# Table columns in PSUM, seven raw and eleven split weight buffers, and a lighter share of the weight splits for GpSimd

## The chip, the cores and the metric

The kernel runs on one core of a Trainium2 chip. The metric is device microseconds of one execution, from the launch of the program on the chip to its end, inputs and outputs in HBM. Before the change three runs took 615.19, 617.08 and 616.91 us, so the median is 616.91 us. The five engines of the core are called by the profile's names: PE (matrix multiply; PEld is its weight load), DVE (vector), ACT (scalar), POOL (GpSimd) and SP (which here only issues DMAs).

## The reference: what is computed

A linear attention feeds a mixture of experts. Cut to what matters:

```
q, k, v: (8 batches, 8 heads, 576 positions, 64); w_phi: (64, 128), all float32
phi(x)  = proj = x @ w_phi; proj -= max|proj| over its 128 features; [exp(proj), exp(-proj)]
attn    = phi(q) @ (phi(k)^T v) / (phi(q) . sum phi(k) + 1e-6)
x       = attn as (4608 tokens, 512)
compute = x @ w_skip > 0            # the other tokens are copied to the output
logits  = x[compute] @ w_gate       # 8 experts; expert = argmax, weight = softmax at the argmax
y       = weight * (relu(x @ w1[expert]) @ w2[expert])      # w1: 512 x 1024, w2: 1024 x 512
out     = x + y for computed tokens, x for the others       # (4608, 512) float32
```

## The kernel before, in words

**First stage, 0 to about 342 us.** The attention, batch after batch. It also writes every token's row with its gate weight to DRAM (`xrows`) and sorts the tokens by expert (one-hot rows `OH`, ranks `RKH`, and position patterns `OP`). The change doesn't touch its code.

**Second stage, the experts.** The tokens of an expert are cut into slots, each a piece of matrix work with its own expert. There are three early full slots "E" of 256 rows (their experts are picked before the last batch is known), full slots "D" of 256 rows, "C" slots of 192 rows and "S" slots of 128 rows, in the order `('E','E','E','C','C','SC','C','DS','C','D')`; in "SC" and "DS" two slots are interleaved. A slot has two layers and each layer's weights come in four **chunks** of 128 x 1024 float32 (512 KB), so there are 96 chunks, numbered 0 to 95 in the order in which PE uses them: 0 to 23 are the three E slots, 24 to 39 two C slots, 40 to 55 the SC pair (40 to 43 the S slot's first layer, 44 and 45 half of the C slot's first layer, 46 to 49 the S slot's second layer, 50 to 55 the rest of C), 56 to 63 a C slot, 64 to 79 the DS pair, 80 to 87 a C slot and 88 to 95 the last D slot.

**The way of one chunk.** (1) `fetch` (L184, L187) issues the DMA on SP's queue into a **raw buffer** `wraw_c`. (2) `split` makes two float32r halves so that PE can multiply at its fast rate without losing accuracy: ACT copies raw to `hi` (L195), then DVE or POOL writes `lo = raw - hi` (L200) into a **split buffer** `w`. DVE does a chunk in one instruction of 1024 columns, POOL in four of 256. (3) PE multiplies with `hi` and `lo`: L932 (hi), L933 (hi with the token's low half `xl`) and L935 (lo) in the first layer of a full slot, L946, L950 (lo) and L951 in its second; L919 and L922 (lo) in a C slot's first layer; L848, L849 (lo), L850 and L869, L870 (lo), L871 in an S slot. There are 11 raw buffers (the first 12 chunks use four of them) and 9 split buffers. A raw buffer is free for the next load when ACT and the `lo` engine have read it, a split buffer when PE has used it.

**Who splits.** ACT makes every `hi`. For `lo`, POOL takes a fixed list of the E chunks (`gp`: 0, 1, 2, 4, 6, 8, 9, 11, 12, 14, 17, 19, 21), chunks 1 and 3 of a C slot's first layer, and chunks 1 and 3 of each layer of an S slot. DVE takes all others. POOL's queue also issues the gathers of token rows (L213) and the scatters of output rows (L879).

**What sets the order.** The code of the second stage stands under a manual schedule: each engine runs in the order of the Python calls. At step k the loop first calls `part` (the split) for all chunks up to a reach of k+5 whose estimated time is due, and after each split the `load` of the chunk 11 further on. Then come PE's matmuls of chunk k, then ReLU and the `hlo` half of the hidden activations (L824 and L825; for C slots L924, L925 `hsum`, L834, L836), and the work that is hung on the step by `at`: the row gathers, the transposes of gathered rows with their halves `xh` (L809) and `xl` (L810), the stores (L893 with the row index L878, L904, L905), and pieces of `tables`. The estimates `ready`, `parted` and `T` only steer this placing.

**The tables.** `tables` computes which token goes to which slot, on DVE, in pieces at the steps 5 to 32. For each of 36 token tiles it has small columns (128 partitions x 36): `pe`, rank `rk`, the three coefficients `cc`, `lt`, and the column `col`. From `col` four comparisons make `eq` (L1061, 128 x 558), and PE multiplies them with `OP` (L1050) to the index table in the PSUM bank K. All of these columns lie in SBUF.

Of the kernel before, what the change touches and what calls it, by code (L numbers as in the profile page):

```python
# [8 lines left out]
F32 = mybir.dt.float32  # L9
F32R = mybir.dt.float32r  # L10
BF16 = mybir.dt.bfloat16
I32 = mybir.dt.int32
AF = mybir.ActivationFunctionType
ALU = mybir.AluOpType
AX = mybir.AxisListType
# [3 lines left out]
P = 128  # L19
# [5 lines left out]
def kernel(  # L25
# [91 lines left out]
    eid0 = const.tile([1, 3], I32, name="eid0")  # L117
    idg0 = const.tile([P, 3, 2], I32, name="idg0")
    pad0 = const.tile([P, 3, 2], I32, name="pad0")
    const.tile([1, 40], I32, name="spare")  # L120
    mark = const.tile([1, 32], I32, name="mark")[:, 0:1]

    ft = const.tile([P, NSL, 4], I32, name="ft")
# [51 lines left out]
    def fetch(which, wap, c):  # L175
        i = nchunk[0]

        j = i % 4 if i < 12 else (i - 8) % 11
        rawp = wpool[0 if j < 4 else 3]
        nchunk[0] += 1  # L180
        raw = rawp.tile([P, 1024], F32, tag="wraw%d" % j, name="wraw_c", bufs=1)
        if which == 1:
            src = wap[:, :, c * FC:(c + 1) * FC].rearrange("o (k p) f -> p (o k) f", p=P)
            nc.sync.dma_start(out=raw.rearrange("p (k f) -> p k f", f=FC), in_=src)  # L184
        else:
            src = wap[:, c * FC:(c + 1) * FC, :].rearrange("o (k p) m -> p (o k) m", p=P)
            nc.sync.dma_start(out=raw.rearrange("p (k m) -> p k m", m=DM), in_=src)  # L187
        return which, i, raw

    def split(chunk, eng):  # L190
        which, i, raw = chunk
        s = i % 9
        pair = wpool[1 if s < 4 else 2].tile([P, 2, 1024], F32R, tag="w%d" % s, name="w", bufs=1)
        hi, lo = pair[:, 0], pair[:, 1]
        nc.scalar.activation(out=hi, in_=raw, func=AF.Copy)  # L195

        n = 256 if eng is nc.gpsimd else 1024
        for a in range(0, 1024, n):
            r = slice(a, a + n)
            eng.tensor_tensor(out=lo[:, r], in0=raw[:, r], in1=hi[:, r].bitcast(F32), op=ALU.subtract)  # L200
        w = FC if which == 1 else DM
        return hi.rearrange("p (k f) -> p k f", f=w), lo.rearrange("p (k f) -> p k f", f=w)
# [761 lines left out]
    start = {"E": 0, "D": 0, "C": NSD, "S": NS2}  # L964

    def tables():
        cn = bank("K")[:, 0:E]
        nc.tensor.matmul(cn, ones_b, Stot, start=True, stop=True)
        yield
        ni = const.tile([P, E], I32, name="ni")  # L970
# [40 lines left out]
        nc.vector.tensor_tensor(out=cf[:, 2], in0=cf[:, 2], in1=cf[:, 1], op=ALU.subtract)  # L1011

        rk = const.tile([P, NT], F32, name="rk")
        pe = const.tile([P, NT], F32, name="pe")
        tm = const.tile([P, NT, E], F32, name="tm")
        cc = const.tile([P, 3, NT], F32, name="cc")
        col = const.tile([P, NT], F32, name="col")
        lt = const.tile([P, NT], F32, name="lt")
        pk = const.tile([P, E], F32, name="pk")

# [8 lines left out]
        nc.vector.tensor_reduce(out=pe, in_=tm, axis=AX.X, op=ALU.add)  # L1029
        nc.vector.scalar_tensor_tensor(out=rk, in0=pe, scalar=-2.0, in1=RKH, op0=ALU.mult, op1=ALU.add)  # L1030
        yield
        for c in range(3):
            nc.vector.tensor_tensor(out=tm, in0=OH, in1=per_e(cf[:, c], NT), op=ALU.mult)
            nc.vector.tensor_reduce(out=cc[:, c], in_=tm, axis=AX.X, op=ALU.add)
        yield
        nc.vector.tensor_tensor(out=lt, in0=rk, in1=cc[:, 1], op=ALU.is_lt)
        nc.vector.tensor_tensor(out=col, in0=cc[:, 0], in1=cc[:, 2], op=ALU.subtract)
        nc.vector.tensor_tensor(out=col, in0=col, in1=lt, op=ALU.mult)
        nc.vector.tensor_tensor(out=col, in0=col, in1=cc[:, 2], op=ALU.add)
        nc.vector.tensor_tensor(out=col, in0=col, in1=rk, op=ALU.add)  # L1040
        nc.vector.scalar_tensor_tensor(out=col, in0=rk, scalar=0.0, in1=col, op0=ALU.is_ge, op1=ALU.mult)
        ix = bank("K")[:, 0:NCOL]
        C = 9
        rxs = []

# [98 lines left out]
    took = {"E": 2.85, "D": 2.85, "C": 2.4, "S": 1.45}  # L1144
    T, ready, parted = [], [], []
    for k, (w, x, c) in enumerate(steps):
        arrive = 0.0 if k < FIRST else max(ready[k - 1] + (3.0 if k < 12 else 2.35), parted[k - (4 if k < 12 else 11)] + 4.0)
        ready.append(arrive)
        parted.append(max(arrive, T[k - 9] + 3.0 if k >= 9 else 0.0, parted[k - 1] + 1.25 if k else 0.0))
        T.append(max(T[k - 1] + took[steps[k - 1][1][0]] + (1.0 if w == 1 and c == 0 else 0.0) if k else 2.0,  # L1150
                     parted[k] + 2.5))

# [39 lines left out]
    with tc.manual_schedule():  # L1192
# [4 lines left out]
        for k, (w, x, c) in enumerate(steps):  # L1197
            kind, i = x
            for f in [f for s, f in before if s == k]:
                f()  # L1200
            tabled[0] = kind != "E"
            todo = [f for s, f in along if s == k]
            while nxt < len(steps) and nxt <= k + 5 and (nxt <= k + 1 or parted[nxt] <= T[k] + 1.0):
                w_, x_, c_ = steps[nxt]
                v = nxt not in CFG["gp"] if x_[0] == "E" else not (
                    (x_[0] == "C" and w_ == 1 or x_[0] == "S") and c_ % 2 == 1)
                part(nxt, nc.vector if v else nc.gpsimd)
                for n in (range(nxt + 4, nxt + 5) if nxt < 7 else range(11, 19) if nxt == 7 else range(nxt + 11, nxt + 12)):
                    load(n)
                nxt += 1  # L1210
            if w == 1:
                if kind == "S":
                    st = hss.setdefault(x, {})
                    half1(wts[k], xss[x], c, st)
                    if c % 2 == 1:
                        st[c // 2] = half1_out(st[c // 2], c // 2)

                        def turn(st=st, g=c // 2):
                            st[g] = half1_turn(st[g])
                        at(k + 1, turn)  # L1220
                else:
                    hss.setdefault(x, []).append(mm1(wts[k], xss[x]))
            else:
                if c == 0:
                    ys[x] = [bank("O") for _ in range(1 if kind == "S" else 2)]
                if kind == "S":
                    half2(wts[k], ys[x][0], hss[x], c)
                elif x != last:
                    mm2(wts[k], ys[x], xss[x], hss[x], c)
                elif c == NFC - 1:  # L1230
                    for sub in range(2):
                        for cc in range(NFC):
# [12 lines left out]
            for s, f in [a for a in along if a[0] == k and a[1] not in todo]:
                f()
# [47 lines left out]
```

## Time and profile before

| | before |
|---|---|
| median of 3 runs | 616.91 us (615.19 to 617.08) |
| the profiled execution, time | 617.51 us |
| the profiled execution, span from first to last instruction | 615.8 us |
| granted TensorE clock, mean | 0.984 |
| attention, about 0 to 342 us; expert slots to the last matmul | PE from 343.1 to 605.8 us |
| PE busy | 571.6 us, 93% |
| DVE, POOL, ACT busy | 509.9, 381.5, 331.0 us |
| weight loads | 96 of 512 KB, median 5.2 us from issue to landing |

How to read it: the span is that of one execution that the profiler recorded, and the execution took 1.7 us more than its span. PE's busy time counts a matmul from start to its modelled end, so that a busy PE is not yet a PE at its peak rate; what an engine waits for is read from the idle times in front of its instructions. In the timeline rows a number stands for the start in us, the next for the duration in us (of all instructions merged in the row, with their count as x4 and the like), then engine, line, operation, the tile written and the tiles read, and shapes; a bracket at the end has the idle time before and what ended it. The duration of a DVE or POOL instruction runs from the end of its semaphore waits, so it contains whatever else holds it up.

### The profile page before, as it was taken

What the parts mean: (1) busy time and instruction counts of PE and PEld (TensorE: products, weight loads), DVE (VectorE), ACT (ScalarE), POOL (GpSimd) and SP (SyncE); (2) the same over time, 40 slices, a digit from 0 to 9 for tenths busy, and PEclk for the clock granted to TensorE, in tenths of its full rate; (3) what the DMA queues carried; (4) which work ended last, traced back from release to release, by engine and by line L of the source; (5) the groups of instructions that cost most, each with busy time, mean ns of one, the idle gap of its engine ahead of it and who ended that gap; (6) DMA issues with size and microseconds to landing.
All of it is one profiled execution on the core that took longest, in us unless ns stands there. A gap on an engine that the chain in (4) does not pass through costs nothing. (4 is left out here: it accounts for less than half of the span.)

```text
span 615.8 us, 18780 instructions
## 1 busy us (share of the span) xinstructions
PE 571.6 (93%) x7486; PEld 467.4 (76%) x7486; DVE 509.9 (83%) x1081; ACT 331.0 (54%) x649; POOL 381.5 (62%) x415
## 2 busy tenths in 40 slices
PE   4899999999999999998899799789999799999993
PEld 2577777767777677776667789588889589989892
DVE  5899999999989999999997679967688877956851
ACT  3465556556655555655544454334658556666620
POOL 5665585494855967667754756855467983559121
PEclk9899999999999999999999899999999899999997
DMA  9998888987677766423153499577686599597200
GB/s 157 160 157 150 186 184 178 196 184 142 134 162 160 160 114 155 119 73 113 37 160 127 136 338 341 170 275 228 216 263 203 178 297 327 175 318 238 76 19 30
DMA packets 250234, 108.34 MB, mean 176 GB/s; under 512 B 192417, under 2 KB 235553, under 8 KB 250144
## 3 DMA queue, kind: packets, MB, share of 16 engines
q1 hardware_dynamic: 245632, 97.58, 60.7%
q0 software_dynamic: 3200, 9.45, 4.5%
q8 instruction: 60, 0.98, 0.7%
q10 hardware_dynamic: 1312, 0.08, 0.1%
q14 instruction: 30, 0.25, 0.1%
HBM read 83.86 MB, written 24.02 MB: 175 GB/s over the span
## 5 line engine op out<-in xcount | busy, mean ns | idle before, releaser
L200 POOL TENSOR_TENSOR w<-wraw_c,w 128x256 fp32r<-128x256 f32 x124 | 109.8, 920 | 42.1 <-ACT w L195 36.0
L380 POOL TENSOR_TENSOR z<-ek 128x512 f32<-128x512 f32 x64 | 81.2, 1273 | 77.0 <-ACT ek L373 54.1
L195 ACT ACTIVATE w<-wraw_c 128x1024 fp32r<-128x1024 f32 x96 | 97.6, 1052 | 3.8 <-DMA wraw_c<-in_moe_w_dram 3.5
L200 DVE TENSOR_TENSOR w<-wraw_c,w 128x1024 fp32r<-128x1024 f32 x65 | 87.8, 1359 | 13.9 <-ACT w L195 12.8
L354 DVE TENSOR_REDUCE m<-ps_P 128x8 f32<-128x1024 f32 (+2 forms) x86 | 88.6, 1030 | 7.1 <-PE ps_P L347 7.1
L357 DVE TENSOR_TENSOR u<-ps_P,m 128x1024 f32<-128x1024 f32 (+2 forms) x86 | 88.8, 1033 | 2.9
L347 PE MATMUL ps_P<-wsrc,xT 64*64 64x128 f32 x2048 | 79.3, 283 | 11.7 <-DMA raw<-in_k_dram 7.1
L513 PEld LDWEIGHTS ps_O<-kva,eq 128*64 128x64 f32 x2048 | 74.0, 136 | 16.3 <-issue 5.8
L513 PE MATMUL ps_O<-kva,eq 128*64 128x74 f32 x2048 | 77.4, 228 | 3.8 <-DVE lgm L476 3.7
L347 PEld LDWEIGHTS ps_P<-wsrc,xT 64*64 64x64 f32 x2048 | 57.4, 135 | 28.2 <-issue 20.3
L399 ACT ACTIVATE eq<-ps_U 128x512 f32<-128x512 f32 x64 | 37.9, 593 | 64.7 <-PE ps_U L393 64.2
L415 PE MATMUL ps_K<-ek,v 128*64 128x256 f32 x512 | 72.0, 400 | 0.0
L879 POOL DMA_INDIRECT out_dram<-o,si x22 | 28.8, 1309 | 66.8 <-DVE si L878 60.4
L946 PE MATMUL ps_O<-w,hh 128*128 128x512 f32 x160 | 64.1, 401 | 0.0
L633 POOL TENSOR_SCALAR OP<-iota_p,rkp,wcol 128x128 bf16<-128x128 f32 x62 | 48.4, 790 | 24.0 <-DVE RKH L636 17.8
L372 ACT ACTIVATE ek<-u 128x512 f32<-128x512 f32 x64 | 40.5, 633 | 38.7 <-DVE u L357 22.8
L950 PE MATMUL ps_O<-w,hh 128*128 128x512 f32 x120 | 47.8, 398 | 3.5 <-DVE w L200 2.9
L393 PE MATMUL ps_U<-ident,u 128*128 128x128 f32 x288 | 48.9, 287 | 1.0 <-DVE u L357 0.6
L324 DVE STREAM_TRANSPOSE xT<-raw 128x512 f32<-128x512 f32 x64 | 44.7, 701 | 5.9 <-PE ps_P L347 2.6
L415 PEld LDWEIGHTS ps_K<-ek,v 128*64 128x64 f32 x512 | 32.1, 138 | 21.5 <-issue 11.3
L951 PE MATMUL ps_O<-w,hlo 128*128 128x512 f32 x120 | 47.6, 397 | 0.1
L384 POOL TENSOR_TENSOR z<-z 128x512 f32<-128x512 f32 x32 | 40.8, 1274 | 2.5
(253 smaller groups left out, 1214.1 us busy)
## 6 DMA issues: line engine op xcount, KB each, us to landing
wraw_c<-in_moe_w_dram SPq DMA_DIRECT2D x96, 512.0 KB, 5.2
raw<-in_k_dram SPq DMA_DIRECT2D x64, 144.0 KB, 3.1
raw<-in_q_dram SPq DMA_DIRECT2D x64, 144.0 KB, 4.1
v<-in_v_dram SPq DMA_DIRECT2D x64, 128.0 KB, 2.8
out_dram<-xm SPq DMA_DIRECT2D x16, 512.0 KB, 4.2
xrows<-xm SPq DMA_DIRECT2D x8, 516.0 KB, 4.1
xrows<-xm SPq DMA_DIRECT2D x8, 512.0 KB, 4.4
vt<-in_v_dram SPq DMA_DIRECT2D x32, 32.0 KB, 2.6
```

What stands on the lines that cost most here:

```text
L195: nc.scalar.activation(out=hi, in_=raw, func=AF.Copy)
L200: eng.tensor_tensor(out=lo[:, r], in0=raw[:, r], in1=hi[:, r].bitcast(F32), op=ALU.subtract)
L347: nc.tensor.matmul(p[s * 64:s * 64 + 64, hd, (nj + j) * NF:(nj + j + 1) * NF], xT[r, g * P + s * 64:g * P + s * 64 + 64], wsrc[r], start=T ...
L354: nc.vector.tensor_reduce(out=m.rearrange("p (j h) -> p j h", h=2), in_=pv, axis=AX.X, op=ALU.max, apply_absolute_value=True)
L357: nc.vector.tensor_tensor(out=uu[:, 0:2 * nj, :].rearrange("p (j h) f -> p j h f", h=2), in0=pv, in1=m.rearrange("p (j h o) -> p j h o", h ...
L380: zeng.tensor_tensor(out=z, in0=e[:, 0:2, :], in1=e[:, 2:4, :], op=ALU.add)
L393: nc.tensor.transpose(t[:, tt * P:(tt + 1) * P], uu[:, tt, :], ident)
L415: nc.tensor.matmul(o[hd * 64:hd * 64 + 64, :], u.v[:, 2 * hd + pr, g * D:(g + 1) * D], u.e[i][:, 2 * j + hd, :], start=(g == 0), stop=False,)
L513: nc.tensor.matmul(ov[s * 64:s * 64 + 64, 2 * j + hd, :], e[:, half, j, hd, s * 64:s * 64 + 64], kva[:, half, 2 * pr + hd, :], start=(half ...
L633: (nc.vector if last else nc.gpsimd).tensor_scalar(out=OP[:, t0 + t, c, :], in0=iota_p, scalar1=rkp[:, t:t + 1], scalar2=wcol[:, NT:NT + 1 ...
L946: nc.tensor.matmul(y[sub], hh[:, t], wh[:, fi, :], start=first, stop=False)
L950: nc.tensor.matmul(y[sub], hh[:, t], wl[:, fi, :], start=False, stop=False)
```

## The change

Four things are changed, in the second stage alone.

1. **Table columns.** `tables` keeps its PSUM bank K for its whole run and places `pe`, `col` and the first two coefficients (`c0`, `c1`, before `cc[:, 0]` and `cc[:, 1]`) in it, next to the counts and the index table. `rk`, `lt` and the third coefficient `c2` stay in SBUF. The operations on them and their order are the same.
2. **Buffers.** Raw buffers go from 11 to 7, split buffers from 9 to 11. The load that follows the split of chunk n is that of chunk n+7 instead of n+11. The memory for both together stays the same (11 x 4 KB + 9 x 8 KB = 7 x 4 KB + 11 x 8 KB = 116 KB in each partition).
3. **Reach.** The split of a chunk may be placed up to six steps ahead of PE instead of five, and the estimates are made for the new numbers of buffers.
4. **Shares.** In an S slot POOL makes `lo` for chunk 1 of each layer only; chunk 3 goes to DVE. With two S slots of two layers that is four chunks of 96.

A spare tile of the constants grows from 40 to 64 words, so that everything behind it lies 512 bytes lower than before.

```diff
@@ fetch, split
-        j = i % 4 if i < 12 else (i - 8) % 11
+        j = i % 4 if i < 12 else (i - 8) % 7
-        s = i % 9
+        s = i % 11
@@ tables
-        cn = bank("K")[:, 0:E]
+        kb = bank("K")
+        cn = kb[:, 0:E]
...
-        pe = const.tile([P, NT], F32, name="pe")
+        ix = kb[:, E:E + NCOL]
+        pe, col, c0, c1 = (kb[:, a:a + NT] for a in range(E + NCOL, E + NCOL + 4 * NT, NT))
         tm = const.tile([P, NT, E], F32, name="tm")
-        cc = const.tile([P, 3, NT], F32, name="cc")
-        col = const.tile([P, NT], F32, name="col")
+        c2 = const.tile([P, NT], F32, name="c2")
...
-        for c in range(3):
+        for c, cc in enumerate((c0, c1, c2)):
             nc.vector.tensor_tensor(out=tm, in0=OH, in1=per_e(cf[:, c], NT), op=ALU.mult)
-            nc.vector.tensor_reduce(out=cc[:, c], in_=tm, axis=AX.X, op=ALU.add)
+            nc.vector.tensor_reduce(out=cc, in_=tm, axis=AX.X, op=ALU.add)
@@ the loop over the steps
-            while nxt < len(steps) and nxt <= k + 5 and (nxt <= k + 1 or parted[nxt] <= T[k] + 1.0):
+            while nxt < len(steps) and nxt <= k + 6 and (nxt <= k + 1 or parted[nxt] <= T[k] + 1.0):
                 v = nxt not in CFG["gp"] if x_[0] == "E" else not (
-                    (x_[0] == "C" and w_ == 1 or x_[0] == "S") and c_ % 2 == 1)
+                    x_[0] == "C" and w_ == 1 and c_ % 2 == 1 or x_[0] == "S" and c_ == 1)
-                for n in (range(nxt + 4, nxt + 5) if nxt < 7 else range(11, 19) if nxt == 7 else range(nxt + 11, nxt + 12)):
+                for n in (range(nxt + 4, nxt + 5) if nxt < 7 else range(11, 15) if nxt == 7 else range(nxt + 7, nxt + 8)):
                     load(n)
```

The order in which the engines run shows where this lands. On DVE, in the stretch of the tables (the first `w` is the split of chunk 13, `hlo` belongs to the second E slot), before:

```order
L1029 TENSOR_REDUCE pe<-tm 128x36
L1030 SCALAR_TENSOR_TENSOR rk<-pe,RKH 128x36
L200 TENSOR_TENSOR w<-wraw_c,w 128x1024
L825 SCALAR_TENSOR_TENSOR hlo<-ps_P,hh 128x512
L1033 TENSOR_TENSOR tm<-OH,cf 128x288
```

and now:

```order
L1030 TENSOR_REDUCE ps_K<-tm 128x36
L1031 SCALAR_TENSOR_TENSOR rk<-ps_K,RKH 128x36
L200 TENSOR_TENSOR w<-wraw_c,w 128x1024
L825 SCALAR_TENSOR_TENSOR hlo<-ps_P,hh 128x512
L1034 TENSOR_TENSOR tm<-OH,cf 128x288
```

No row moves here, nor in the rest of this stretch up to the last `eq`: the same operations follow each other, and only where a column is read and written changes.

On POOL, in the SC pair, before (a row `w` is a chunk of four pieces: 41 and 43, behind the two scatters L879 45, and behind the two gathers L213 47, 49 and 51):

```order
L200 TENSOR_TENSOR w_7715<-wraw_c_7368,w_7715 128x256 x4
L200 TENSOR_TENSOR w_7758<-wraw_c_7438,w_7758 128x256 x4
L879 DMA out_0_dram<-o_7791,si_7793 4608x512
L888 MEMSET mark_129 1x1
L879 DMA out_0_dram<-o_7800,si_7804 4608x512
L888 MEMSET mark_129 1x1
L200 TENSOR_TENSOR w_7810<-wraw_c_7500,w_7810 128x256 x4
L213 DMA xg_7874<-xrows_93,ft_130 128x514
L213 DMA xg_7876<-xrows_93,ft_130 64x514
L200 TENSOR_TENSOR w_7878<-wraw_c_7548,w_7878 128x256 x4
L200 TENSOR_TENSOR w_7927<-wraw_c_7615,w_7927 128x256 x4
L200 TENSOR_TENSOR w_8005<-wraw_c_7685,w_8005 128x256 x4
```

and now (chunks 41, 45, 47 and 51):

```order
L200 TENSOR_TENSOR w_7676<-wraw_c_7468,w_7676 128x256 x4
L200 TENSOR_TENSOR w_7767<-wraw_c_7576,w_7767 128x256 x4
L879 DMA out_0_dram<-o_7785,si_7787 4608x512
L888 MEMSET mark_129 1x1
L879 DMA out_0_dram<-o_7794,si_7798 4608x512
L888 MEMSET mark_129 1x1
L200 TENSOR_TENSOR w_7837<-wraw_c_7646,w_7837 128x256 x4
L213 DMA xg_7859<-xrows_93,ft_130 128x514
L213 DMA xg_7861<-xrows_93,ft_130 64x514
L200 TENSOR_TENSOR w_7960<-wraw_c_7755,w_7960 128x256 x4
```

Chunks 43 and 49 have left POOL, and chunk 45 stands before the two scatters, chunk 47 before the two gathers; each stood behind them. On DVE chunks 43 and 49 stand behind chunks 42 and 48, and from chunk 22 on a split stands in front of the work of the step before the one in which it stood (before, DVE ran split 46 behind the two `xl` of the C slot of the pair, now ahead of them).

More of the change, by code (lines that the diff above doesn't have):

```diff
@@ L119 @@
     pad0 = const.tile([P, 3, 2], I32, name="pad0")
-    const.tile([1, 40], I32, name="spare")
+    const.tile([1, 64], I32, name="spare")
     mark = const.tile([1, 32], I32, name="mark")[:, 0:1]
@@ L1031, in tables @@
         yield
-        for c in range(3):
+        for c, cc in enumerate((c0, c1, c2)):
             nc.vector.tensor_tensor(out=tm, in0=OH, in1=per_e(cf[:, c], NT), op=ALU.mult)
-            nc.vector.tensor_reduce(out=cc[:, c], in_=tm, axis=AX.X, op=ALU.add)
+            nc.vector.tensor_reduce(out=cc, in_=tm, axis=AX.X, op=ALU.add)
         yield
-        nc.vector.tensor_tensor(out=lt, in0=rk, in1=cc[:, 1], op=ALU.is_lt)
-        nc.vector.tensor_tensor(out=col, in0=cc[:, 0], in1=cc[:, 2], op=ALU.subtract)
+        nc.vector.tensor_tensor(out=lt, in0=rk, in1=c1, op=ALU.is_lt)
+        nc.vector.tensor_tensor(out=col, in0=c0, in1=c2, op=ALU.subtract)
         nc.vector.tensor_tensor(out=col, in0=col, in1=lt, op=ALU.mult)
-        nc.vector.tensor_tensor(out=col, in0=col, in1=cc[:, 2], op=ALU.add)
+        nc.vector.tensor_tensor(out=col, in0=col, in1=c2, op=ALU.add)
         nc.vector.tensor_tensor(out=col, in0=col, in1=rk, op=ALU.add)
         nc.vector.scalar_tensor_tensor(out=col, in0=rk, scalar=0.0, in1=col, op0=ALU.is_ge, op1=ALU.mult)
-        ix = bank("K")[:, 0:NCOL]
         C = 9
@@ L1146 @@
     for k, (w, x, c) in enumerate(steps):
-        arrive = 0.0 if k < FIRST else max(ready[k - 1] + (3.0 if k < 12 else 2.35), parted[k - (4 if k < 12 else 11)] + 4.0)
+        arrive = 0.0 if k < FIRST else max(ready[k - 1] + (3.0 if k < 12 else 2.35), parted[k - (4 if k < 12 else 7)] + 4.0)
         ready.append(arrive)
-        parted.append(max(arrive, T[k - 9] + 3.0 if k >= 9 else 0.0, parted[k - 1] + 1.25 if k else 0.0))
+        parted.append(max(arrive, T[k - 11] + 3.0 if k >= 11 else 0.0, parted[k - 1] + 1.25 if k else 0.0))
         T.append(max(T[k - 1] + took[steps[k - 1][1][0]] + (1.0 if w == 1 and c == 0 else 0.0) if k else 2.0,
```

## The prediction

> **What bounds the kernel now.** I read the page's sums first, then who PE waits for in the expert stage, then busy time and clock by stretch, then the timelines of PE, DVE and POOL where PE waits.
>
> ```profile
> span 615.8 us, 18780 instructions
> PE 571.6 (93%) x7486; PEld 467.4 (76%) x7486; DVE 509.9 (83%) x1081; ACT 331.0 (54%) x649; POOL 381.5 (62%) x415
> ```
>
> PE is the bound as a whole, so only time in which it waits or runs at a lower clock can be won. PE's waits from 320 us on (total us, times, longest):
>
> ```profile
> PE ps_O L870 <- POOL w L200: 3.2, 3, 1.4
> PE ps_O L950 <- DVE w L200: 2.9, 1, 2.9
> PE ps_P L919 <- DVE hsum L925: 2.1, 4, 1.0
> PE ps_P L933 <- DVE x L810: 1.7, 1, 1.7
> PE ps_O L950 <- POOL w L200: 0.6, 1, 0.6
> PE ps_P L935 <- POOL w L200: 0.5, 2, 0.3
> PE ps_P L922 <- POOL w L200: 0.3, 1, 0.3
> ```
>
> They lie in two places. Busy time by stretch (us, PE, PEld, DVE, ACT, POOL, then the granted clock):
>
> ```profile
> 380.00:392.00 12.00, 10.87 (x53) 8.48 (x52) 11.76 (x14) 5.22 (x6) 11.51 (x14) 1.00 0.72 224
> 392.00:404.00 12.00, 7.30 (x31) 5.39 (x30) 11.90 (x14) 2.98 (x4) 6.34 (x7) 0.86 0.54 176
> 468.00:480.00 12.00, 11.68 (x91) 11.15 (x90) 10.61 (x14) 9.50 (x17) 11.47 (x14) 1.00 0.63 203
> 480.00:496.00 16.00, 12.79 (x58) 10.26 (x59) 13.55 (x16) 7.73 (x12) 15.51 (x15) 0.89 0.65 218
> ```
>
> In 380 to 404 us, the tables, DVE has not half a microsecond to spare. In 480 to 496, the SC pair, it is POOL. In both the clock falls behind the waits: 12 x 0.14 = 1.7 us and 16 x 0.11 = 1.8 us lost. Now the tables' stretch, on DVE, POOL and PE:
>
> ```profile
> 378.54 5.57 DVE L1030 SCALAR_TENSOR_TENSOR rk<-pe,RKH 128x36 f32<-128x36 f32 x1
> 384.03 1.21 DVE L200 TENSOR_TENSOR w<-wraw_c,w 128x1024 fp32r<-128x1024 f32 x1
> 389.23 0.68 DVE L825 SCALAR_TENSOR_TENSOR hlo<-ps_P,hh 128x512 fp32r<-128x512 f32 x1
> 389.82 0.33 DVE L1036 TENSOR_TENSOR lt<-rk,cc 128x36 f32<-128x36 f32 x1
> 392.97 0.66 DVE L1041 SCALAR_TENSOR_TENSOR col<-rk,col 128x36 f32<-128x36 f32 x1
> 393.66 1.19 DVE L1061 TENSOR_TENSOR eq<-i,col 128x558 bf16<-128x558 f32 x1
> 394.77 1.75 DVE L200 TENSOR_TENSOR w<-wraw_c,w 128x1024 fp32r<-128x1024 f32 x1
> 397.04 0.72 DVE L1061 TENSOR_TENSOR eq<-i,col 128x558 bf16<-128x558 f32 x1
> 401.78 1.28 DVE L810 TENSOR_TENSOR x<-ps_U,x 128x512 fp32r<-128x512 f32 x2
> ...
> 378.48 5.57 POOL L200 TENSOR_TENSOR w<-wraw_c,w 128x256 fp32r<-128x256 f32 x8
> 387.41 10.93 POOL L200 TENSOR_TENSOR w<-wraw_c,w 128x256 fp32r<-128x256 f32 x12
> ...
> 396.57 0.50 PE L950 MATMUL ps_O<-w,hh 128*128 128x512 f32 x1 [2.92 <-DVE w L200]
> 403.12 0.38 PE L933 MATMUL ps_P<-x,w 128*128 128x256 f32 x1 [1.68 <-DVE x L810]
> ```
>
> An operation on 36 columns needs 5.57 us, as long as POOL's eight pieces (chunks 11 and 12) run, and ends with them. From 389.82 to 393.66 six such operations take 3.84 us, 0.64 each, with POOL's pieces beside them (10.93 / 12 = 0.91 each). The split of chunk 15 (394.77) is late by this, PE waits 2.92 us for it, and `xl` of the third slot (401.78) is late next. Every slow operation reads two operands in SBUF; `hlo`, which reads ps_P, stays at 0.68.
>
> **Part 1, the columns.** Two rows give the price of a small operation without such a wait, one with a PSUM operand and one with SBUF operands:
>
> ```profile
> 368.93 0.14 DVE L980 SCALAR_TENSOR_TENSOR cl<-pks,ps_K 128x8 f32<-128x8 f32 x1
> 370.62 0.17 DVE L984 SCALAR_TENSOR_TENSOR rm_e<-nn,cl 128x8 f32<-128x8 f32 x1
> ```
>
> Writing a small column to PSUM isn't shown; I bound it by 0.14 and, for a whole 128x512 from PSUM, 0.68, and take 0.2 with the pause between dependent operations. `rk` then reads one SBUF operand instead of two: 5.57 - 0.2 = 5.4 us. The six operations from `lt` to the last `col`: 3.84 - 6 x 0.2 = 2.6. The first `eq`: 1.19 - 0.72 = 0.5. In all DVE is free 8.5 us earlier.
>
> [...]
>
> What this is worth on PE is less. The next on DVE is split 13, which has two SBUF operands and now meets POOL's eight pieces at about 378.8 instead of 384.03. Taking turns, as chunk 15's split did, it costs 1.75 instead of 1.21, and pushes POOL's chunk 11 by about 1.2 us, for which PE already waits. So of PE's waits here (2.9 + 1.7 + 0.6 + 0.5 = 5.7) the first two go; those for POOL stay (1.1) and grow by 1.2: 5.7 - 2.3 = **3.4 us**. Without a wait of 2.9 us I take the clock to stay up: **1.7 us**. Together 5.1; the ends are 7.4 (nothing stays) and 2.8 (below, split 13 held for all eight pieces).
>
> **Part 2, the S slots.** The prices of a chunk, and the places:
>
> ```profile
> L200 POOL TENSOR_TENSOR w<-wraw_c,w 128x256 fp32r<-128x256 f32 x124 | 109.8, 920 | 42.1 <-ACT w L195 36.0
> L200 DVE TENSOR_TENSOR w<-wraw_c,w 128x1024 fp32r<-128x1024 f32 x65 | 87.8, 1359 | 13.9 <-ACT w L195 12.8
> 464.79 7.59 POOL L200 TENSOR_TENSOR w<-wraw_c,w 128x256 fp32r<-128x256 f32 x8 [6.66 <-ACT w L195]
> 475.91 3.89 POOL L200 TENSOR_TENSOR w<-wraw_c,w 128x256 fp32r<-128x256 f32 x4
> 482.90 12.66 POOL L200 TENSOR_TENSOR w<-wraw_c,w 128x256 fp32r<-128x256 f32 x12
> 472.92 1.01 DVE L810 TENSOR_TENSOR x<-ps_U,x 128x512 fp32r<-128x512 f32 x2
> 475.64 0.86 PE L919 MATMUL ps_P<-x,w 128*128 128x384 f32 x4
> ```
>
> A chunk costs POOL 4 x 0.92 = 3.7 us and DVE 1.36. POOL's last row is chunks 47, 49 and 51; PE waits for the first two (3.2 us) and before for 45 (0.3). Now POOL has 41 and 45 in the place of 41 and 43, and 47 in the place of 45: 47 ends near 480 (475.91 + 3.89) instead of 487 (482.90 + a third of 12.66), and 51 follows the gathers. No `lo` of POOL is late: 3.5 + 1.8 of clock = 5.3 us at most. DVE gets chunks 43 and 49, 2.4 to 3.5 us in a stretch where it was busy 10.6 of 12. Queued behind is `xl` of the C slot, ahead of which split 46 now stands too: it ended at 473.9 and PE uses it at 475.64, so 1.7 us of margin meet up to 2 x 1.75 = 3.5, a loss of 0 to 1.8; the same again for `hsum`, on which PE's next PSUM bank hangs. Splits run one step earlier and DVE meets fewer pieces of POOL, so I take 0.7 for each: 5.3 - 1.4 = **3.9 us**, ends 5.3 and 1.7. In the DS pair PE waits for no split and nothing is won.
>
> **Part 3, the buffers.** They are costed at nothing, hidden by the lead of the loads:
>
> ```profile
> ACT w L195 <- DMA wraw_c<-in_moe_w_dram: 3.5, 3, 2.4
> DMA to landing us min/median/max: 3.4/5.2/10.3
> L195 ACT ACTIVATE w<-wraw_c x96: 1042/1051/1077, 338.1 to 589.7; 128x1024 fp32r<-128x1024 f32 x96
> 474.13 0.36 PE L848 MATMUL ps_P<-w,x 128*128 128x256 f32 x1
> ```
>
> In the whole expert stage ACT waited 3.5 us for raw weights, so the loads run ahead. A raw buffer is now taken again 7 chunks later, and is busy for the landing (5.2 us), ACT's copy (1.05) and at most POOL's 3.7: 9.95 / 7 = 1.4 us a chunk. PE's fastest chunks, those of an S slot, take 475.64 - 474.13 = 1.5 us. That is little room, but S chunks come in runs of two to four and splits stand some steps ahead; if that cover is gone, the price is rival D. Eleven split buffers remove a wait that PE's list doesn't show, and add none: a split at reach k+6 needs the buffer of chunk k-5, long used.
>
> The sum: 3.4 + 1.7 + 3.9 = 9.0 us off the profiled span, 615.8 - 9.0 = 606.8. With the 1.7 us that lie around the span, 608.5; the profiled execution was 0.6 above the median of the runs, so **607.9 us**.
>
> **The rivals.**
>
> *A: the block moves to split 13.* `rk` waited through eight pieces and not one, at the same place where split 13 will now ask. If it is held in the same way, it ends at 385.2 as before; only the 2.6 + 0.5 us behind it are won. Split 15 then ends about 393.4, just in time for PE, and `xl` at 403.06 - 3.1 = 400.0, which PE, earlier by 2.9, waits for: 2.8 us in place of 5.1. The time is 607.9 + 2.3 = 610.2. For it: `rk` itself, 0.06 us behind POOL's start. Against it: chunk 15's split (1.75) and the six columns, which got their turn after one piece. [...]
>
> *B: PSUM doesn't help.* The operations would be slow for another reason than the place of their operands (the dependence from one to the next, say). Only part 2 is left: 616.9 - 3.9 = 613.0. Against it: `rm_e<-nn,cl`, with the same dependence, took 0.17.
>
> *C: DVE becomes the bound in the SC pair.* Both margins are overrun by their full bounds: 1.8 for `xl`, 1.8 for `hsum`, and the clock falls as it did (1.8): the 5.3 us are gone. The time is 607.9 + 3.9 = 611.8. For it: DVE's 10.6 of 12 us.
>
> *D, slower: seven raw buffers starve the splits.* ACT works in order; a raw that isn't there when its copy is due holds up the `hidden` copies behind it, and through them PE's banks. By the loop above it decides from a landing of 7 x 1.5 - 4.75 = 5.8 us in the S runs. At the longest landing, 10.3 us, a chunk takes 15.05 / 7 = 2.15 us, 0.65 more than PE's 1.5; over 16 S chunks 10.3 us, with nothing won in part 2: 616.9 - 5.1 + 10.3 = 622.1. For it: the median is close to 5.8. Against it: the loads in the S runs share the DMA queues with less (DMA share 0.63 to 0.65 in the rows of 468 to 496 is not full: their last numbers, 203 and 218, are GB/s), and the chunks that are split early are no longer needed at once.
>
> **How the numbers follow.** The forecast 0.5, A 0.2, B 0.1, C 0.1, D 0.1. The forecast's own range is from the ends of parts 1 and 2, 616.9 - 12.7 = 604.2 to 616.9 - 2.8 - 1.7 = 612.4. The range for 8 of 10 takes in A, C and B and leaves out most of D: 603.5 to 614.5. Less than 0.3% (1.85 us) is about what a measurement of this kernel can't tell from no change: faster means under 615.1, slower over 618.8. The forecast, A, B and C are faster, but for a tail of about 0.06 in which their gains come out small; D is slower except for a part of 0.03 that ends near no change: faster 0.84, same 0.09, slower 0.07.
>
> **What would show it.** In the profile after: `rk` at about 0.2 us and the five `col` operations near 0.2 each; split 13 starting before 380 us, at 1.75 us (forecast) or over 4 (A); PE's waits for L200 by DVE and for L810 in the tables gone, and the clock of 392 to 404 near 1.00; no wait of L870 for POOL in the SC pair, and its clock near 1.00. ACT's waits for raw weights tell of D: under 6 us in all if I am right, over 15 if D. I am wrong if `rk` is fast and the span doesn't move: then something else, `xl` or a gather, was due at the same time.

## The result, and the profile after

The changed kernel took 608.95 us (median of 4 runs, 607.91 to 610.47) beside 617.0 us for the kernel before (4 runs): a ratio of 0.9871, with a 95% interval of 0.9843 to 0.9899. In a second comparison it took 607.62 us (6 runs) beside 616.23 us, 0.9863 (0.9834 to 0.9891). The forecast was 607.9 us. The total is right, and, as the experiments show, for reasons that are in good part not those of the forecast.

The profiled execution took 607.91 us. Its page begins, and two of its groups read (busy us, mean ns of one, idle before):

```profile
span 605.7 us, 18767 instructions
PE 567.1 (94%) x7486; PEld 466.3 (77%) x7486; DVE 502.6 (83%) x1085; ACT 330.7 (55%) x649; POOL 375.9 (62%) x399
...
L200 POOL TENSOR_TENSOR w<-wraw_c,w 128x256 fp32r<-128x256 f32 x108 | 97.5, 935 | 47.5 <-ACT w L195 43.9
L200 DVE TENSOR_TENSOR w<-wraw_c,w 128x1024 fp32r<-128x1024 f32 x69 | 90.2, 1321 | 9.5 <-ACT w L195 7.6
```

Four chunks have gone from POOL to DVE (124 - 108 = 16 pieces; 69 - 65 = 4). What PE waits for from 320 us on:

```profile
PE ps_P L919 <- DVE hsum L925: 2.4, 4, 1.1
PE ps_P L935 <- POOL w L200: 2.1, 3, 0.9
PE ps_U L806 <- DVE x L810: 1.6, 1, 1.6
PE ps_P L932 <- ACT x L809: 1.4, 1, 1.4
```

The waits for the split of chunk 15 (L950, 2.9 us), for `xl` (L933, 1.7 us) and for POOL in the SC pair (L870, 3.2 us) are gone. The stretches of the tables and of the SC pair, busy us of PE, PEld, DVE, ACT, POOL and then the granted clock:

```profile
380.00:392.00 12.00, 9.90 (x45) 8.16 (x45) 11.62 (x22) 5.71 (x7) 11.51 (x12) 0.86 0.52 176
392.00:404.00 12.00, 11.90 (x131) 10.45 (x129) 7.18 (x11) 5.70 (x7) 11.61 (x13) 1.00 0.75 257
468.00:480.00 12.00, 12.00 (x79) 11.23 (x78) 9.99 (x14) 9.72 (x17) 11.32 (x14) 1.00 0.62 215
480.00:496.00 16.00, 16.00 (x87) 13.89 (x87) 14.28 (x22) 10.14 (x17) 8.64 (x9) 1.00 0.94 321
496.00:520.00 24.00, 22.15 (x135) 20.15 (x134) 20.34 (x35) 14.68 (x25) 12.66 (x14) 1.00 0.78 267
```

In 480 to 496 PE now runs without a gap and at full clock. In 496 to 520 it doesn't: there it waits for `hsum` of DVE, 1.09 and 0.76 us. And the clock of the tables has not been mended: the drop stands one stretch earlier, at 0.86 in 380 to 392. DVE's timeline in the tables, and the PE rows behind which the clock falls:

```profile
379.13 0.20 DVE L1031 SCALAR_TENSOR_TENSOR rk<-ps_K,RKH 128x36 f32<-128x36 f32 x1
379.25 1.74 DVE L200 TENSOR_TENSOR w<-wraw_c,w 128x1024 fp32r<-128x1024 f32 x1
384.92 0.18 DVE L1037 TENSOR_TENSOR lt<-rk,ps_K 128x36 f32<-128x36 f32 x1
386.09 0.20 DVE L1042 SCALAR_TENSOR_TENSOR ps_K<-rk,ps_K 128x36 f32<-128x36 f32 x1
386.98 1.22 DVE L200 TENSOR_TENSOR w<-wraw_c,w 128x1024 fp32r<-128x1024 f32 x1
...
381.62 0.38 PE L935 MATMUL ps_P<-x,w 128*128 128x256 f32 x1 [0.92 <-POOL w L200]
382.58 0.38 PE L935 MATMUL ps_P<-x,w 128*128 128x256 f32 x1 [0.58 <-POOL w L200]
383.56 0.39 PE L935 MATMUL ps_P<-x,w 128*128 128x256 f32 x1 [0.60 <-POOL w L200]
```

`rk` takes 0.20 us instead of 5.57, the column operations 0.18 to 0.20, split 13 takes its turn at 1.74 us, and split 15 starts at 386.98 instead of 394.77. Laid side by side, the two profiles seem to confirm part 1 of the forecast to the letter. The experiments show that they don't.

### The profile page after: what moved, and what is told of

The parts are those of the page before. It is cut to its first block, busy times and chain, and to the rows that moved or that the text cites. A ratio compares the mean times of both kernels' runs of the same rounds, so it can differ in the third digit from the quotient of the medians.

```text
span 605.7 us, 18767 instructions
## 1 busy us (share of the span) xinstructions
PE 567.1 (94%) x7486; PEld 466.3 (77%) x7486; DVE 502.6 (83%) x1085; ACT 330.7 (55%) x649; POOL 375.9 (62%) x399
## 5 line engine op out<-in xcount | busy, mean ns | idle before, releaser
L200 POOL TENSOR_TENSOR w<-wraw_c,w 128x256 fp32r<-128x256 f32 x108 | 97.5, 935 | 47.5 <-ACT w L195 43.9
L200 DVE TENSOR_TENSOR w<-wraw_c,w 128x1024 fp32r<-128x1024 f32 x69 | 90.2, 1321 | 9.5 <-ACT w L195 7.6
L879 POOL DMA_INDIRECT out_dram<-o,si x22 | 34.3, 1558 | 56.6 <-DVE si L878 50.1
L950 PE MATMUL ps_O<-w,hh 128*128 128x512 f32 x120 | 47.2, 394 | 0.1
```

Source lines behind the costliest of these rows:

```text
L950: nc.tensor.matmul(y[sub], hh[:, t], wl[:, fi, :], start=False, stop=False)
```

## The experiments

All ratios are to the kernel before in the same comparison.

### One part at a time

Four kernels, of which the first three are the kernel before with one edit each. Columns alone (with the spare tile of 64 words):

```diff
-        cn = bank("K")[:, 0:E]
+        kb = bank("K")
+        cn = kb[:, 0:E]
...
+        ix = kb[:, E:E + NCOL]
+        pe, col, c0, c1 = (kb[:, a:a + NT] for a in range(E + NCOL, E + NCOL + 4 * NT, NT))
...
```

> The kernel before with the table columns in PSUM alone (11 raw and 9 split buffers, reach k+5, old shares). [...] Rival (the slow operations come from the dependence of one on the next): rk and the columns stay slow, within 0.5 us of before.

Shares alone:

```diff
-                    (x_[0] == "C" and w_ == 1 or x_[0] == "S") and c_ % 2 == 1)
+                    x_[0] == "C" and w_ == 1 and c_ % 2 == 1 or x_[0] == "S" and c_ == 1)
```

> The kernel before with the new shares alone (POOL splits one of four chunks of an S slot's layer). As the prediction put it (POOL has too much to split in the SC pair): 3.9 us faster (1.7 to 5.3), PE's 3.2 us of waits for L870 gone. Rival, read from the order of this kernel on POOL: chunk 45 still stands behind the two scatters and chunk 47 behind the two gathers, whose issue waits for DVE's row index, so both are as late as before and only the wait for chunk 49 (1.2 us) with a little of the clock goes: 1.2 to 2 us faster, with 2 us of waits for L870 left.

Buffers, planner's numbers and reach together, with the loads seven chunks ahead instead of eleven:

```diff
-        j = i % 4 if i < 12 else (i - 8) % 11
+        j = i % 4 if i < 12 else (i - 8) % 7
...
-        s = i % 9
+        s = i % 11
...
-            while ... nxt <= k + 5 and ...
+            while ... nxt <= k + 6 and ...
...
```

> The kernel before with 7 raw and 11 split buffers, reach k+6 and the load 7 ahead, but SBUF columns and old shares. As the prediction put it (the buffers are worth nothing by themselves): within 1 us of before, the waits for L870 as before or moved. Rival (the reach does the work): on POOL chunk 45 now stands ahead of the scatters and chunk 47 ahead of the gathers, so that their lateness goes with the reach and not with the shares: 3 to 5 us faster, waits for L870 under 1 us, with POOL still splitting chunks 43 and 49. Slower rival (seven raw buffers starve the splits): ACT waits for raw weights over 15 us in all and the time is above before.

And the changed kernel without the columns in PSUM (the first edit taken back):

> The changed kernel with the table columns back in SBUF. Additive parts: slower than the change by what the columns give alone, 5.1 us by the prediction (2.8 to 7.4), so 3 to 6 us faster than before, with the waits of the tables' stretch as before (split 15 2.9, xl 1.7) and those of the SC pair gone. Rival (the parts cover each other: eleven split buffers already take the late split 15 up): the columns give less than 2 us here.

| kernel | median, us | before, us | ratio, 95% |
|---|---|---|---|
| columns alone | 615.70 (12 runs) | 616.06 | 0.999 (0.9965 to 1.0014) |
| shares alone | 614.04 (12) | 616.06 | 0.9962 (0.9938 to 0.9986) |
| buffers, planner, reach | 611.44 (10) | 616.06 | 0.9913 (0.9885 to 0.9942) |
| changed, without columns | 609.72 (6) | 616.06 | 0.9895 (0.9853 to 0.9937) |

The columns, the largest term of the forecast (5.1 us), win 0.4 us by themselves, which can't be told from nothing. The edit that was costed at nothing wins 4.6. Without the columns 6.3 us of the gain are still there.

The trace of the shares says why. Its program is the same as before, instruction for instruction on every engine, up to the SC pair at about 460 us. Yet chunk 17 comes 27.3 us after chunk 10, where the first profile of before has 31.9. DVE and POOL in that kernel, where the columns still lie in SBUF:

```profile
378.72 0.83 DVE L1030 SCALAR_TENSOR_TENSOR rk<-pe,RKH 128x36 f32<-128x36 f32 x1
379.48 1.81 DVE L200 TENSOR_TENSOR w<-wraw_c,w 128x1024 fp32r<-128x1024 f32 x1
...
378.67 7.50 POOL L200 TENSOR_TENSOR w<-wraw_c,w 128x256 fp32r<-128x256 f32 x8
```

`rk` starts 0.05 us behind POOL's first piece, much as it did before (378.54 behind 378.48), and takes 0.83 us. The 5.57 us, and with them the waits of 2.9 and 1.7 us, may have belonged to the one execution that was profiled.

### The kernel before, profiled again

> The kernel before, profiled once more. Theory now: the 5.57 us of rk belonged to one execution. With the split shares alone (columns still in SBUF, the same program on every engine up to the SC pair) rk started 0.05 us behind POOL's first piece, as before, and took 0.83 us, and the chunks behind it were 4.6 us earlier. So here: rk about 0.8, the split of chunk 13 about 1.8 us and before 380 plus the shift, no wait of PE for the split of chunk 15 by DVE (under 0.5 us), chunk 17 about 4.5 us earlier from chunk 10 on than in the first profile (27 us instead of 32). Rival (the prediction): the hold is what this program does; rk 5.57 again, waits of 2.9 and 1.7 us, 32 us from chunk 10 to chunk 17.

This execution took 616.47 us. `rk` and split 13 on DVE, all that PE waited for from 320 us on, and two stretches with their clock (0.86 and 0.82):

```profile
379.87 0.83 DVE L1030 SCALAR_TENSOR_TENSOR rk<-pe,RKH 128x36 f32<-128x36 f32 x1
380.62 1.81 DVE L200 TENSOR_TENSOR w<-wraw_c,w 128x1024 fp32r<-128x1024 f32 x1
...
PE ps_P L922 <- POOL w L200: 2.8, 3, 1.3
PE ps_P L919 <- DVE hsum L925: 2.0, 3, 1.0
PE ps_P L935 <- POOL w L200: 1.9, 2, 1.3
PE ps_U L806 <- DVE x L810: 1.6, 1, 1.6
PE ps_O L870 <- POOL w L200: 1.6, 2, 1.2
PE ps_P L932 <- ACT x L809: 1.4, 1, 1.4
PE ps_O L950 <- POOL w L200: 0.6, 1, 0.6
...
380.00:392.00 12.00, 10.11 (x51) 8.76 (x50) 11.66 (x21) 5.94 (x7) 11.53 (x12) 0.86 0.59 209
480.00:496.00 16.00, 12.71 (x53) 10.30 (x54) 13.55 (x14) 6.27 (x10) 10.54 (x12) 0.82 0.56 194
```

No wait of L950 for DVE, no wait of L933 for `xl`. In the eight profiles that were taken with the columns in SBUF, `rk` took 5.57 us once, 0.82 to 0.83 six times and 0.38 once (there it began ahead of POOL's pieces). The theory holds: the tables' waits of the first profile were an accident of that execution, and the change can't win back in the median what the median doesn't lose. The tables of this execution and of the changed kernel cost the same, as the pace of PE shows (us from the first matmul of chunk 10 to that of the chunk named, read from PE's timeline):

| kernel (one profiled execution each) | 17 | 46 | 52 | 60 | 91 |
|---|---|---|---|---|---|
| before, first profile | 31.9 | 105.0 | 120.8 | 140.5 | 215.7 |
| before, second profile | 27.4 | 99.3 | 116.9 | 138.1 | 213.3 |
| columns alone | 26.5 | 99.7 | 112.2 | 136.3 | 211.4 |
| shares alone | 27.3 | 99.8 | 114.0 | 135.6 | 210.2 |
| reach alone (below) | 26.6 | 99.0 | 109.1 | 133.7 | 208.4 |
| changed, without columns | 27.4 | 99.9 | 110.0 | 131.5 | 206.2 |
| changed | 27.3 | 98.9 | 108.9 | 130.6 | 205.3 |

Of the seven profiles that are not in this table six have chunk 17 at 26.3 to 28.3 us, and that of buffers, planner and reach together has it at 29.0; the long `rk` is in none of them.

Against the second profile of before the changed kernel wins 0.1 us up to chunk 17 (the tables), 0.4 up to 46, and 8.0 up to 52: 7.6 us in the SC pair alone (17.6 us for chunks 46 to 51 become 10.0). Of this 0.5 is lost up to chunk 60.

That the first profile was only 1.5 us over the 616 us that is usual here, though its tables cost 4.5 us more than those of the second, is the work of the other stretches. Its chunk 10 came 1.3 us earlier (376.2 against 377.5), chunks 17 to 45 took 1.2 us more, chunks 46 to 51 of the SC pair 1.8 less (15.8 against 17.6), and 52 to 59 another 1.5 less (19.7 against 21.2).

The time in front of chunk 10, where the programs don't differ, moves from execution to execution, and so does the clock there. In the execution with the columns alone chunk 10 came at 378.9. Clock and stretch of the first profile of before, and of the columns alone:

```profile
20.00:30.00 10.00, 7.88 (x123) 4.93 (x124) 8.22 (x13) 4.79 (x12) 5.73 (x5) 0.83 0.86 155
```

```profile
20.00:30.00 10.00, 7.66 (x90) 4.87 (x90) 7.42 (x11) 4.51 (x11) 5.55 (x5) 0.66 0.98 173
300.00:320.00 20.00, 18.30 (x283) 13.55 (x282) 19.34 (x57) 10.08 (x24) 12.20 (x11) 0.91 0.35 107
340.00:360.00 20.00, 16.86 (x168) 16.23 (x163) 12.59 (x32) 10.32 (x16) 12.09 (x16) 0.83 0.60 176
```

And of the changed kernel:

```profile
20.00:30.00 10.00, 5.93 (x119) 4.12 (x122) 8.04 (x12) 4.50 (x12) 5.34 (x5) 1.00 0.87 156
```

In 20 to 30 us the clock fell short by 10 x 0.17 = 1.7 us in the first, 10 x 0.34 = 3.4 in the second, and by nothing in the third. In the first the trace has the clock at 0.50 from 22.4 to 25.4 us, at 0.71 and 0.78 in the 0.4 us on either side of that, and at 1.00 from 25.8 on.

This loss alone doesn't say when chunk 10 comes: with none of it the changed kernel has it at 376.6, with 1.7 us the first profile of before at 376.2. The columns alone, where it came late, lost more behind it: 20 x 0.09 = 1.8 us and 0.08 more than the first profile of before in 340 to 360 (0.83 for 0.91), 20 x 0.08 = 1.6. The 1.3 us between the two profiles of before are not of the clock: both have 0.83, 1.00 and 0.91 in these three stretches. Where they come from was not found.

### Buffers or reach

The reach alone, on the kernel before:

```diff
-            while ... nxt <= k + 5 and ...
+            while ... nxt <= k + 6 and ...
```

> The kernel before with the reach of the splits at k + 6 instead of k + 5, and nothing else: eleven raw and nine split buffers, two of four S chunks for POOL, columns in SBUF. On POOL it gives the same order as the kernel with the buffers, the planner's numbers and the reach together. Theory: the reach does the work of that edit (POOL splits chunks 43 and 47 ahead of scatters and gathers): 611.4 us within 1.5, no wait of L870 for POOL over 0.5 us. Rival: the eleven split buffers do it: 616 within 1.

On POOL it is chunk 45, not the 43 of this expectation, that stands ahead of the scatters.

The buffers and the planner's numbers without it (the first two edits of the third kernel above, with the loads seven chunks ahead):

> The kernel before with seven raw and eleven split buffers and the planner's numbers for them, but the reach still at k + 5; the order on POOL is that of before. Theory: the buffers are worth nothing, 616 us within 1 (the prediction too costs them at nothing). Rival: the split buffers carry the 4.6 us: about 611.4. A loss of 2 us or more would be the prediction's rival D in small: raw buffers come back too late.

The changed kernel with the old buffers, eleven raw and nine split, and the new reach:

> The changed kernel with eleven raw and nine split buffers as before, and the reach still at k + 6; the columns and the shares as changed. The order on DVE, ACT and POOL is that of the changed kernel. Theory: the buffers are worth nothing by themselves, the gain of that edit is the reach: a ratio to before of 0.987 within 0.003, as the changed kernel's 0.986 to 0.987. Rival: the two more split buffers let ACT and DVE write earlier; without them PE waits for splits again and 2 us or more of the 8 are lost (0.990 or more). Five raw and twelve split buffers gave 0.995.

And the changed kernel with the raw buffers cut further, the loads five chunks ahead:

```diff
-        j = i % 4 if i < 12 else (i - 8) % 7
+        j = i % 4 if i < 12 else (i - 8) % 5
...
-        s = i % 11
+        s = i % 12
...
```

> The changed kernel with five raw and twelve split buffers instead of seven and eleven, each load issued five chunks ahead. It takes the prediction's rival D further: by its loop a chunk needs (5.2 + 1.05 + 3.7) / 5 = 2.0 us, over the 1.5 us of PE's S chunks. If the loop decides, 16 S chunks times 0.5 us are lost: about 617 us, and ACT waits over 10 us for raw weights. If the splits' lead over PE covers it, within 1.5 us of the changed kernel: 608 to 610.5.

| kernel | median, us | before, us | ratio, 95% |
|---|---|---|---|
| reach alone | 611.68 (12 runs) | 615.07 | 0.9958 (0.9936 to 0.9979) |
| buffers alone | 615.10 (12) | 615.07 | 1.0006 (0.9979 to 1.0033) |
| changed, old buffers | 607.86 (6) | 616.39 | 0.9862 (0.982 to 0.9904) |
| changed, five raw buffers | 611.47 (12) | 615.07 | 0.995 (0.9931 to 0.997) |

The buffers are worth nothing that shows, on the kernel before (by the interval between 1.3 us faster and 2.0 slower) and under the changed one (2.6 us either way). The reach wins 3.4 us alone by the medians, 2.6 by the ratio: with it POOL splits chunk 45 ahead of the two scatters and 47 ahead of the two gathers. (By its ratio it is somewhat less than the 0.9913 of buffers, planner and reach together; the intervals overlap, on every engine the two kernels run the same instructions in the same order, and the two rows of the buffers show nothing that makes up the rest.) Seven raw buffers are enough, five are not. ACT's waits for raw weights with five:

```profile
ACT w L195 <- DMA wraw_c<-in_moe_w_dram: 17.3, 16, 3.0
```

They were 3.5 us before and are 6.5 in the changed kernel (4.6 in its second profile). Every engine runs the same instructions in the same order as in the changed kernel, so the loss is that of the buffers. This costs 2.5 to 3.9 us by the medians (611.47 against 608.95 and 607.62), 4.9 by the ratios (0.995 - 0.987, of 616): the starved ACT of rival D, at about half of the 8 us that its loop gives for five buffers. Through which of PE's waits it comes was not followed.

### What the SC pair loses: POOL's run holds up DVE

Why do shares and reach each help, and more together? A part is as the forecast has it: with the shares alone PE still waits for chunks 45 and 47 behind scatters and gathers (0.3 us at L922, 2.1 at L870), and with the reach alone not at all. The rest is on DVE. The same operation of DVE, the `hlo` of the C slot behind chunk 45 (L836, two operands in SBUF, 0.43 us when nothing holds it), stands just behind POOL's first pieces after the gathers in most profiles. With the columns alone, where POOL has chunks 47, 49 and 51 in one run:

```profile
480.29 8.36 POOL L200 TENSOR_TENSOR w<-wraw_c,w 128x256 fp32r<-128x256 f32 x12
480.61 8.32 DVE L836 SCALAR_TENSOR_TENSOR hlo<-hsum,hh 128x256 fp32r<-128x256 f32 x1 [0.59 <-ACT hh L834]
493.26 0.50 PE L946 MATMUL ps_O<-w,hh 128*128 128x512 f32 x1 [1.32 <-DVE o L893]
```

With the reach alone, where 47 has moved ahead and the run is 49 and 51:

```profile
478.39 5.61 POOL L200 TENSOR_TENSOR w<-wraw_c,w 128x256 fp32r<-128x256 f32 x8
478.71 5.57 DVE L836 SCALAR_TENSOR_TENSOR hlo<-hsum,hh 128x256 fp32r<-128x256 f32 x1 [0.59 <-ACT hh L834]
489.75 0.50 PE L946 MATMUL ps_O<-w,hh 128*128 128x512 f32 x1 [2.43 <-DVE o L893]
```

In the changed kernel, where 49 is DVE's and the run is 51 alone:

```profile
477.39 2.83 POOL L200 TENSOR_TENSOR w<-wraw_c,w 128x256 fp32r<-128x256 f32 x4
477.71 2.80 DVE L836 SCALAR_TENSOR_TENSOR hlo<-hsum,hh 128x256 fp32r<-128x256 f32 x1 [0.59 <-ACT hh L834]
```

The operation starts 0.32 us behind POOL in these three and ends with POOL's run: after twelve, eight and four pieces. Everything on DVE behind it waits as long. It isn't always so. In the first profile of before it also started 0.32 us behind the first of twelve pieces, and was let in after three:

```profile
483.22 2.17 DVE L836 SCALAR_TENSOR_TENSOR hlo<-hsum,hh 128x256 fp32r<-128x256 f32 x1 [0.59 <-ACT hh L834]
```

In the changed kernel without the columns it started later, 1.01 us behind POOL's first piece (479.20 behind 478.19), and took 2.11, again to the end of POOL's run (481.03). With twelve and with eight pieces the splits and the `o` behind it come too late for PE (1.32 and 2.43 us); with four, in the profile shown, they don't (in its second one PE waits 0.7 us for `o`). So the shares and the reach seem to do more than bring `lo` earlier: they shorten the run that can hold DVE. A hold need not cost PE time: in the second profile of before a split at 472.25 us took 3.77 us, through POOL's four pieces from 472.10 on, and PE waited for no split of DVE. All this is read from traces; a kernel with the same order on DVE and POOL and the hold taken away was not tried.

In the second profile of before it was another operation, a split, that was held by the eight pieces of 47 and 49:

```profile
478.38 5.57 POOL L200 TENSOR_TENSOR w<-wraw_c,w 128x256 fp32r<-128x256 f32 x8
478.57 6.46 DVE L200 TENSOR_TENSOR w<-wraw_c,w 128x1024 fp32r<-128x1024 f32 x1 [0.20 <-ACT w L195]
```

The chain from there to PE can be followed. Behind the split `hsum` ends late on DVE, and ACT waits for it 6.62 us in front of its `hh`. ACT's next five `hi` stand behind that, and POOL waits for one of them before it begins chunk 51:

```profile
487.15 4.76 POOL L200 TENSOR_TENSOR w<-wraw_c,w 128x256 fp32r<-128x256 f32 x4 [3.20 <-ACT w L195]
```

PE waits 2.8 us for these pieces (L922, above). Behind the hold the clock fell to 0.82 in 480 to 496, which is 16 x 0.18 = 2.9 us.

### The columns once more, and chunk 11

> The changed kernel once more, beside the kernel without columns in PSUM and in the same call, to price the columns. Theory: rk is held for 5.57 us only now and then (in one of seven profiles with the columns in SBUF so far), so the median gains under 1 us by them: this run 0 to 1.2 us under the one without. Rival (the prediction's part 1): 5.1 us. Against before 0.987 to 0.989.

> The changed kernel with the columns back in SBUF (the other two parts stay). Theory: 0 to 1.2 us over the changed kernel in the same call, rk 0.83 us in the profile; if the rare case is met, rk near 5.5 and the chunks behind it 4.5 us later in that execution. Rival (the prediction's part 1): 5.1 us over it.

Then the changed kernel with chunk 11's `lo` on DVE, since PE's last wait for POOL (2.1 us) is for that chunk:

```diff
- 'gp': (0, 1, 2, 4, 6, 8, 9, 11, 12, 14, 17, 19, 21)
+ 'gp': (0, 1, 2, 4, 6, 8, 9, 12, 14, 17, 19, 21)
```

> The changed kernel with chunk 11's low half split by DVE instead of POOL. In the changed kernel PE waits 2.1 us for three of POOL's pieces of chunk 11, which POOL starts at 379.07 behind two scatters, and the clock of 380 to 392 is 0.86 (1.7 us). DVE would split it at about 377 in 1.2 us. Theory: both go, 2 to 3.8 us faster than the changed kernel of the same call, no L935 wait for POOL over 0.3 us. Rival: the tables, 1.2 us later on DVE, or split 13 become late; then within 1 us of the changed kernel.

| kernel | median, us | before, us | ratio, 95% |
|---|---|---|---|
| changed, again | 607.62 (6 runs) | 616.23 | 0.9863 (0.9834 to 0.9891) |
| changed, without columns, again | 609.55 (6) | 616.23 | 0.9891 (0.9871 to 0.991) |
| changed, chunk 11 on DVE | 607.85 (5) | 616.23 | 0.986 (0.9837 to 0.9884) |

With the rest of the change in place the columns win 1.9 us here (0.8 between the first two comparisons, 609.72 to 608.95): more than the 0 to 1.2 that I had expected, far less than 5.1, and not settled closer than that, since the intervals overlap. No profile of these met the long `rk`. What the traces do show is POOL. Without the columns (first row and wait), with them (second row and wait):

```profile
388.70 11.69 POOL L200 TENSOR_TENSOR w<-wraw_c,w 128x256 fp32r<-128x256 f32 x10
...
PE ps_O L950 <- POOL w L200: 1.5, 2, 1.2
```

```profile
388.53 11.56 POOL L200 TENSOR_TENSOR w<-wraw_c,w 128x256 fp32r<-128x256 f32 x12
...
PE ps_O L950 <- POOL w L200: 0.4, 1, 0.4
```

In the same time POOL does ten pieces or twelve, 1.17 or 0.96 us each: the `eq` comparisons of DVE, which read `col` at the same time, seem to hold up POOL's pieces when `col` lies in SBUF. Two more profiles agree: twelve pieces here took 13.05 us with the shares alone, where the columns lie in SBUF, and 11.55 in the first profile of the changed kernel. PE waits 1.1 us less for them. A part of the columns' gain, perhaps all of it, comes by this way, which the forecast didn't have.

Chunk 11 on DVE wins nothing, although PE comes to chunk 16 at 393.8 us, 17.6 us after chunk 10 instead of 22.4:

```profile
392.00:404.00 12.00, 9.27 (x90) 8.58 (x89) 9.19 (x13) 4.33 (x5) 9.68 (x13) 0.72 0.85 283
...
396.78 0.58 PE L933 MATMUL ps_P<-x,w 128*128 128x256 f32 x1 [2.73 <-DVE x L810]
```

All 4.8 us are given back before chunk 17 (28.3 us after chunk 10, against 27.3): `xl` is due earlier and stands on DVE behind two splits and two `eq`, PE waits 2.73 us for it, and in 392 to 404 the clock is 0.72 (12 x 0.28 = 3.4 us). The tables' stretch has a second limit right behind POOL's chunk 11: DVE, up to `xl`.

## Why the prediction was right or wrong

**The total was right**: 607.9 us forecast, 608.95 and 607.62 measured. It was right by luck, by two errors of opposite sign: 3 to 5 us too much for the columns, some 2.5 too little for the rest. Against the one profile from which it was read both parts fit: the changed kernel's tables took 4.6 us less (31.9 to 27.3), its chunks 46 to 59 3.8 less (35.5 to 31.7).

**Part 1, the columns, was mis-sized: 5.1 us forecast, 0.4 measured alone, 0.8 to 1.9 with the rest.** The step that failed is the one in which PE's waits in the tables (2.9 + 1.7) and the clock behind them were taken for the program's; the waits were one execution's, in one of eight profiles. The prices were right (`rk` 0.20, the columns 0.18 to 0.20, split 13 at 1.74 before 380 us) and DVE is indeed free 7.8 us earlier than in the first profile (split 15 at 386.98 for 394.77). But in the second profile of before DVE is not late either. The clock's 1.7 us were not won: the drop follows PE's wait for POOL's chunk 11, which the forecast left in place (2.1 us; it had said 1.1 + 1.2), and it stands at 0.86 in 380 to 392 in the second profile of before as well as after the change. Such a wait doesn't bring it on in every execution: the changed kernel without the columns has 0.86 there in one profile and 1.00 in the other, with 1.9 and 1.7 us of waits for chunk 11.

**The correction from the profiled execution to the median was the wrong tool.** The forecast took 0.6 us off, since the execution took 617.51 us and the median was 616.91. The execution differed from the second one by +4.5 us in the tables, +1.2 from there to the SC pair, -1.8 in the pair, -1.5 behind it and -1.3 in front of chunk 10; the small difference of the sums hid it.

**Part 2, the shares with the reach's order, was mis-sized the other way: 3.9 us forecast, 6.3 and 6.7 measured** (changed without columns, against before). The mechanism stood: chunk 47 ends before the gathers, L870 doesn't wait, the clock of 480 to 496 is 1.00. The term counted only what the first profile showed, 3.5 us of waits and 1.8 of clock. It lacked the other form of the loss, which the second profile of before has: POOL's run holds DVE for 6.46 us, and PE waits 2.8 us at L922 for it. With 1.6 us for L870 and 2.9 of clock that is 7.3 us, close to the 7.6 that the SC pair won. And the first profile was a cheap execution here: against its 35.5 us for chunks 46 to 59 the changed kernel won 3.8, close to the forecast's 3.9, against the 38.8 of the second profile 7.1. So this term too has the size of the one execution from which it was read. The price at `xl` didn't come; that at `hsum` did, behind the pair: the waits there are 1.09 + 0.76 us, where 0.7 was taken and 1.8 was the bound.

**Part 3, the buffers, was right: nothing that shows**, in two kernels. The reach, though, is worth some 3 us alone; the forecast had used its order within part 2 without a price of its own.

**The rivals.** A didn't come about: split 13 took its turn. B's reason didn't hold, since the PSUM operations take 0.2 us, but its outcome for part 1, next to nothing won, did. C is there in small, as `hsum`. D needs five buffers; with seven ACT's waits rose from 3.5 to 6.5 us (4.6 in a second profile), around the 6 that the forecast had set as the mark, at no cost that the comparison with eleven buffers shows.

The test that the forecast named for itself, "`rk` is fast and the span doesn't move", would have found it only in the kernel with the columns alone: there it is just what happened.

## What to carry to other kernels

A stall that one profile shows at a place where two engines contend may be that execution's alone; before a term of several us is built on it, profile the same kernel again, and ask which of its waits are in both. A small difference between the profiled execution and the median doesn't show that its waits are typical ones, as several large ones can cancel. And where GpSimd runs long trains of small instructions beside DVE, look at their length as well as at their share: shorter trains, placed earlier, won 6 us here, quicker DVE operations 0.4 to 1.9. That the length costs by itself was read from the traces and not tested.

## What the runs showed of the hardware that was not expected

A DVE operation with two operands in SBUF that starts beside a train of GpSimd pieces mostly gets its turn after one piece: in the first profile of before and in that of the changed kernel this holds for all 19 splits of the expert stage that started up to 0.25 us behind the start of a piece. They took 1.60 to 1.77 us; the shortest splits take 1.20 to 1.21. But some operations are held through three or more pieces, most of these to the last piece of the train: 5.57 us (`rk`, eight pieces, first profile of before), 6.46 (a split, eight, second profile), 8.32 (`hlo`, twelve, columns alone), 5.57 (`hlo`, eight, reach alone). A split that began 0.61 us ahead of a train was slow too: it took 2.53 us and ended 1.16 behind the first piece (531.38, first profile of before). While it held `rk`, POOL ran at 5.57 us for its eight pieces, and at 7.50 when DVE took its turns. What decides whether a train lets DVE in was not found: 0.05 us behind POOL's first piece `rk` got its turn (0.82 to 0.83 us: the shares alone, the second profile of before, the changed kernel without the columns, second profile), at 0.07 it was held; `hlo` at 0.32 behind a piece was held through three pieces or more in four profiles (before, columns alone, reach alone, changed), two splits of the changed kernel at 0.29 and 0.30 got their turn after one (1.53 and 1.59 us).
